# A linear-attention block and a gated mixer on one core: where two weight loads stand in the transfer queue

## The chip, the cores and the metric

The kernel runs on one core of a Trainium2 chip. It is a program for five engines that run side by side: PE (TensorE) multiplies matrices, ACT (ScalarE) evaluates functions, DVE (VectorE) works on elements, POOL (GpSimd) does small things, and SP (SyncE) issues nearly all the transfers between the chip's memory (HBM) and the core's own memory (SBUF). Engines wait for each other, and for transfers, through semaphores. The metric is the device time of one execution in microseconds, the median over the runs.

## The reference

```
h  = x + A(layernorm(x))
h2 = h + B(layernorm(h))

A:  q, k, v = x @ wqkv            # 32 heads of 16
    phi(t)  = where(t > 0, t + 1, exp(t)) + 1e-6
    kv = phi(k)^T v ;  z = sum over tokens of phi(k)      # per head
    out = (phi(q) kv / (phi(q) z + 1e-6)) @ wo

B:  z  = gelu(x @ w_in)           # w_in: 512 x 1792
    z1, z2 = the two halves of z  # 896 each
    g  = w_sp @ layernorm(z2) + b_sp     # w_sp: 2048 x 2048, mixes tokens
    out = (z1 * g) @ w_out        # w_out: 896 x 512
```

There are 2048 tokens of width 512, in bf16. The four loads that matter below are `w_in` (win, 1792 KB), `w_out` (wout, 896 KB), and the mixing weights `w_sp`, which are read transposed in 64 pieces of 128 KB.

## The kernel before

The tokens are split in 16 tiles of 128. Stage one normalises the tiles of x and transposes them: most of the transposes are transfers (`dma_t`, L673), named tx0 to tx15 after the tile. PE makes k from each pair of tiles (L756, called k4, k5 and so on), multiplies phi(k) with the normalised tile (L766) and makes q in between (L858). Stage two finishes A: it folds kv and wo in one matrix and multiplies with phi(q) (L903). Stage three normalises h, transposes it by transfers (th0 to th15, L673 again), and multiplies with win: L959 gives z2 by token tile, with its GELU on ACT (L966 or, for the tiles 0, 4, 8 and 12, L974, called g2.n), and L1013 gives z1 transposed. Stage four mixes the tokens (`mix`, L1052): for each quarter tg of the output tokens and each of 7 blocks fc of features, 16 matmuls sum over the 16 tiles of input tokens. It multiplies the result with z1 on DVE. `project` (L1072) multiplies with wout, and DVE adds h and SP stores.

The mixing weights come as transposing transfers (`load_wsp`, L1032). A piece wsp tg.st belongs to quarter tg of the output tokens and tile st of the input tokens. Quarter 0 has a semaphore for each four tiles, so that mix0.0 can go in four parts; each other quarter has one semaphore for its 16 pieces, and the first mix of that quarter waits for all of them. In `mix`, every matmul group but those of mix0.0 waits for all 16 pieces of its quarter before its first matmul. In PE's list the first such group is mix0.2.

The order of the work on each engine is not written out. `Program.schedule` is a list scheduler: it goes through the operations with an estimate of each one's duration, and on each engine takes the ready operation with the least start time plus half its `want`, a due time that comes from the table WANT (L358), one number for each operation in the order in which `build` makes them. `waits` then derives the semaphore waits. So each engine runs a fixed list in order, and an operation that waits holds up everything behind it on its engine. SP's list holds loads, transposes and stores in one queue.

In this list wout stands behind the token transpose tx8 and win behind tx15. In between and behind them stand pieces of wsp and tx12 to tx15:

```
tx8, wout, wsp0.2, tx12, tx13, tx14, tx15, win, wsp0.5, wsp0.3, wsp0.7, wsp0.4, wo, wv, ...
... th8, wsp0.14, wsp1.4, wsp0.9, wsp0.15, wsp0.10, wsp0.8, wsp1.0, wsp0.12, wsp3.10, ...
```

Of the kernel before, what the change touches and what calls it, by code (L numbers as in the profile page):

```python
# [10 lines left out]
P = 128  # L11
# [81 lines left out]
class Program:  # L93
# [306 lines left out]
def build(nc, A_x, A_wqkv, A_wo, B_w_in, B_w_sp, B_b_sp, B_w_out, out):  # L400
# [76 lines left out]
    zw = small([KD, GRAIN], BF16)  # L477
    ones = small([32], BF16)
    eps = small([4], FP32)
    mhalf = small([TPG], FP32)  # L480
    msq = small([TPG], FP32)

# [34 lines left out]
    def act_c(n, ps=True, ptr=0):  # L517
        d = (0.171 if ps else 0.2) + 0.000833 * n + 0.093 * ptr
        return d - 0.1, d + SEM
# [26 lines left out]
    for p in range(1, NP):  # L546
        load("sp", f"x{2 * p}", x[2 * p:2 * p + 2, :],
             x_dram[2 * p * P:(2 * p + 2) * P, :].rearrange("(n p) d -> p n d", p=P), 2 * P * D * 2, -28 + p)


    op("pool", pool_c(0.2), lambda e: e.memset(ident.all().ap(), 0.0), w=[ident.all()], want=-50)
# [87 lines left out]
    def T1(n):  # L639
        return 5.2 + 1.85 * n  # L640

    rs1, cT = {}, {}
    for grp in LN1:
        rs = small([len(grp)], FP32)
        nm = small([len(grp)], FP32) if any(n in ACT_NORM1 for n in grp) else None
        for n in grp:
            stats(x[n, :], Row(st_x, n), T1(n) - 4, f"st{n}")
            aggr(Row(st_x, n), 6, T1(n) - 4, f"ag{n}")
        lo, hi = grp[0], grp[-1] + 1
        for n in grp:  # L650
            if n in LATE:
                d, m = xc[n].all(), st_x[n, 6:7]
                cT[n] = Tile(XC)
                op("dve", dve_f(512), lambda e, n=n, d=d, m=m: e.tensor_scalar(d.ap(), x[n, :].ap(), m.ap(), None,
                                                                              op0=ALU.subtract),
                   r=[x[n, :], m], w=[d, cT[n]()], want=T1(n) - 3, name=f"xc{n}")
        rstd_act(st_x[lo:hi, 7], rs.all(), T1(lo) - 2.5, f"rs{lo}")
        if nm is not None:
            minus_mean(st_x[lo:hi, 6], rs.all(), nm.all(), T1(lo) - 2.5, f"nm{lo}")
        for i, n in enumerate(grp):  # L660
            rs1[n] = rs[i:i + 1]
            if n in ACT_NORM1:
                normalise_act(xn[n, :], x[n, :], nm[i:i + 1], rs[i:i + 1], T1(n) - 2, f"xn{n}")
            else:
                normalise(xn[n, :], x[n, :], st_x[n, 6:7], rs[i:i + 1], T1(n) - 2 + 4 * (n in LATE), f"xn{n}")
    load("sp", "wq", wqkv[:, 0:D], w3[:, :, 0:D], D * D * 2, 27)
    load("sp", "wv", wqkv[:, 2 * D:3 * D], w3[:, :, 2 * D:3 * D], D * D * 2, 30)
    load("sp", "wo", wo.all(), A_wo.rearrange("(c p) f -> p c f", p=P), D * D * 2, 30.1)
    load("sp", "win", win.all(), B_w_in.rearrange("(c p) f -> p c f", p=P), D * F * 2, 30.2)
    load("sp", "wout", wout.all(), B_w_out.rearrange("(c p) f -> p c f", p=P), FH * D * 2, 30.3)  # L670

    def dma_t(a, d, want, name):
        op("sp", (1.31, 2.75), lambda e: e.dma_start_transpose(d.ap(), a.ap()), r=[a], w=[d], dma=(name, False),  # L673
# [216 lines left out]
            op("dve", dve_2(1024), lambda e, r_=r_, d=d: e.tensor_tensor(d.ap(), d.ap(), r_.ap(), ALU.mult),  # L890
               r=[d, r_], w=[d], want=wd + 2, name=f"sc{gq}.{h}")

    hn_t, hn_op = {}, {}
    for p in range(NP):
        t = Tile(PS, 2)
        for ti in range(2):
# [24 lines left out]
    for grp in LN2:  # L921
# [8 lines left out]
        for i, n in enumerate(grp):  # L930
# [3 lines left out]
            else:  # L934
                hn_op[n] = normalise(t(), x[n, :], st_h[n, 6:7], rs[i:i + 1], w0 + 1 + 0.1 * i, f"hn{n}")

    def TZ(p):
        return T0 + 16 + 6 * p

    for p in range(NP):  # L940
# [11 lines left out]
        for n in (2 * p, 2 * p + 1):  # L952
            t = Tile(PS, 2)
            l = hT[:, n * P:(n + 1) * P]

            def mm(e, t=t, l=l):
                for i, (a, b) in enumerate(((FH, FH + 512), (FH + 512, F))):
                    for c in range(KD):
                        k = e.matmul(t(bank(i)).ap()[:, 0:b - a], lhsT=l.ap()[:, c, :], rhs=win[c, a:b].ap(),  # L959
                                     start=(c == 0), stop=(c == KD - 1))  # L960
                return k
            op("pe", pe_c(*([512] * 4 + [FH - 512] * 4)), mm, r=[l, win[:, FH:F]], w=[t()], want=TZ(p) + n % 2, name=f"z2.{n}",
               after=dens if n >= 2 else ())
            d = gz2[n, :]
            if n in ACT_Z:
                op("act", (act_c(FH)[0] + 0.1, act_c(FH)[1] + 0.1), lambda e, t=t, d=d, n=n: e.activation(  # L966
                    d.ap(), t(flat).ap()[:, 0:FH], ACT.Gelu_apprx_tanh, accum_out=st_z[n, 14:15].ap()), r=[t()],
                   w=[d, st_z[n, 14:15]], want=TZ(p) + 1.5, after=lnexp, name=f"g2.{n}")
                j = Tile(JK)
                op("act", (act_c(FH, ps=False)[0] + 0.1, act_c(FH, ps=False)[1] + 0.1), lambda e, d=d, n=n, j=j: e.activation(  # L970
                    j().ap(), d.ap(), ACT.Square, accum_out=st_z[n, 15:16].ap()), r=[d], w=[j(), st_z[n, 15:16]],
                   want=TZ(p) + 2, name=f"sq{n}")
            else:
                op("act", act_c(FH), lambda e, t=t, d=d: e.activation(d.ap(), t(flat).ap()[:, 0:FH], ACT.Gelu_apprx_tanh),  # L974
                   r=[t()], w=[d], want=TZ(p) + 1.5, after=lnexp, name=f"g2.{n}")
                for i, (a, b) in enumerate(((0, 512), (512, FH))):
                    s6, src = st_z[n, 6 * i:6 * i + 6], gz2[n, a:b]
                    op("dve", (0.057 + (b - a) / 985.0, 0.157 + (b - a) / 985.0 + SEM),
                       lambda e, s6=s6, src=src: e.bn_stats(s6.ap(), src.ap()), r=[src], w=[s6], want=TZ(p) + 2.5,
                       name=f"stz{n}")  # L980
                aggr(Row(st_z, n), 12, TZ(p) + 2.5, f"agz{n}")
# [43 lines left out]
    for tg in (0, 2):  # L1025
        z1_unit([(tg, KF - 1), (tg + 1, KF - 1)], z1T[KF - 1, tg * GW:(tg + 2) * GW], Z0 + 8 + tg, f"z1.{KF - 1}.{tg}")


    def load_wsp(tg, want):
        for st in range(NT):  # L1030
# [147 lines left out]
```

## Time and profile before

| | us |
|---|---|
| median of 3 runs | 242.39 |
| lowest and highest run | 242.1 and 243.06 |
| the profiled execution | 242.13 |
| its span in the trace | 240.4 |
| PE busy | 235.1 |
| DVE busy | 127.4 |
| ACT busy | 83.4 |

The span runs from the first to the last instruction of the program; what the execution took beyond it lies around the program. Busy time is the union of an engine's instructions. In a list by line, L1052 is line 1052 of the kernel; operands stand as out<-in. The timeline merges neighbouring instructions of one kind and gives their start, their length and their count; for SP, whose rows are marked SPq, the length is what the issue took, not the transfer. When a transfer is complete is given by its time from issue to landing. `wsp`, `wout`, `win`, `hT` and so on are stores in SBUF; `wqkv_wsp` holds first wqkv and wo and later the fourth quarter of the mixing weights, `k_xn_z` first k and the normalised tiles and later z2, and `xT_pq_z` first the transposed tokens and later z1.

### The profile page before, as it was taken

How to read it: one execution, taken by the hardware profiler on the slowest of the kernel's cores; microseconds unless marked ns; L12 is line 12 of the kernel's file. 1: busy time of each engine (PE TensorE's matmuls, PEld its weight loads, DVE VectorE, ACT ScalarE, POOL GpSimd, SP SyncE). 2: the span in 40 equal slices, each digit the busy share in tenths (PEclk: the TensorE clock that was granted, in tenths of full speed). 3: DMA queues.
4: the chain of work that ended last, by engine and by line, in shares of the span. 5: the costliest groups of instructions: out<-in, count | busy, mean ns of one | idle time of the engine just before them, and what ended most of it. 6: DMA issues, size and time to landing. Idle time of an engine off the chain costs nothing.

```text
span 240.4 us, 3056 instructions
## 1 busy us (share of the span) xinstructions
PE 235.1 (98%) x1177; PEld 108.6 (45%) x1199; DVE 127.4 (53%) x270; ACT 83.4 (35%) x131; POOL 14.2 (6%) x33
## 2 busy tenths in 40 slices
PE   8999999999999999999999999999999999999996
PEld 2444445444444544444444444444444444444443
DVE  5999756299999983227212333324333433332443
ACT  4898965566065799994211100000000000000000
POOL 3000000001202160213000000000000000000000
PEclk9999999999999999999999999999999999999999
DMA  6986789632632545445444544452200001000022
GB/s 195 292 206 81 206 199 313 225 102 95 173 84 56 88 100 107 91 99 100 99 97 104 83 99 108 93 107 66 87 0 0 25 22 44 0 3 0 0 87 87
DMA packets 61805, 24.18 MB, mean 101 GB/s; under 512 B 52064, under 2 KB 61152, under 8 KB 61792
## 3 DMA queue, kind: packets, MB, share of 16 engines
q1 hardware_dynamic: 61648, 23.97, 41.2%
q8 instruction: 9, 0.15, 0.3%
q10 hardware_dynamic: 144, 0.03, 0.1%
q14 instruction: 4, 0.03, 0.1%
HBM read 7.47 MB, written 2.10 MB: 40 GB/s over the span
## 4 chain that ended last, share of the span: by engine, by line
PE 94%; DVE 3%; ACT 1%; issue 1%
PE ps L1052 40%; PE ps L1072 10%; PE ps L959 10%; PE ps L1013 10%; PE ps L903 6%; PE ps L766 6%; PE ps L756 5%; PE ps L858 4%; PE ps L575 2%; DVE hT L802 1%; DVE k_xn_z L837 1%; DVE xT_pq_z L890 0%; PE ps L684 0%; DVE xT_pq_z L725 0%; PE ps L778 0%
## 5 line engine op out<-in xcount | busy, mean ns | idle before, releaser
L1052 PE MATMUL ps<-wsp,k_xn_z 128*128 128x512 bf16 x328 | 73.6, 379 | 0.4
L1058 DVE TENSOR_TENSOR e<-ps,e 128x512 bf16<-128x512 f32 x28 | 19.4, 691 | 69.2 <-PE ps L1052 69.2
L1052 PEld LDWEIGHTS ps<-wsp,k_xn_z 128*128 128x128 bf16 x336 | 32.9, 98 | 39.7
L1013 PE MATMUL ps<-hT,win 128*128 128x512 bf16 x110 | 26.0, 379 | 0.1
L959 PE MATMUL ps<-win,hT 128*128 128x384 bf16 (+1 forms) x126 | 25.3, 352 | 0.1
L1072 PE MATMUL ps<-wout,xT_pq_z 128*128 128x512 bf16 (+2 forms) x125 | 25.1, 355 | 0.1
L1052 PE MATMUL ps<-wqkv_wsp,k_xn_z 128*128 128x512 bf16 x110 | 24.2, 379 | 0.1
L1018 ACT ACTIVATE xT_pq_z<-ps 128x1024 bf16<-128x1024 f32 x14 | 14.1, 1021 | 25.5 <-PE ps L1013 25.5
L587 DVE BATCH_NORM_STATS2 small<-xh 128x6 f32<-128x512 bf16 x32 | 21.0, 679 | 3.0 <-DMA xh<-in_A_x_dram 2.9
L959 PEld LDWEIGHTS ps<-win,hT 128*128 128x128 bf16 x128 | 12.5, 98 | 12.4
L1072 PEld LDWEIGHTS ps<-wout,xT_pq_z 128*128 128x128 bf16 x126 | 11.8, 98 | 12.7
L1052 PEld LDWEIGHTS ps<-wqkv_wsp,k_xn_z 128*128 128x128 bf16 x112 | 11.0, 98 | 13.2
L1013 PEld LDWEIGHTS ps<-hT,win 128*128 128x128 bf16 x112 | 11.0, 98 | 12.6
L1076 DVE TENSOR_TENSOR e<-ps,xh 128x512 bf16<-128x512 f32 (+2 forms) x18 | 11.3, 632 | 9.7 <-PE ps L1072 9.2
L714 ACT ACTIVATE e<-ps 128x1024 bf16<-128x1024 f32 (+1 forms) x16 | 15.4, 970 | 2.0 <-PE ps L756 1.1
L766 PE MATMUL ps<-k_xn_z 128*128 128x512 bf16 x63 | 15.2, 379 | 0.2 <-issue 0.2
L858 PE MATMUL ps<-xT_pq_z,wqkv_wsp 128*128 128x512 bf16 x61 | 15.0, 379 | 0.1
L903 PE MATMUL ps<-k_xn_z,xT_pq_z 128*128 128x512 bf16 x62 | 14.0, 379 | 0.6 <-DVE k_xn_z L837 0.4
L966 ACT ACTIVATE k_xn_z<-ps 128x896 bf16<-128x896 f32 x12 | 10.9, 909 | 9.2 <-PE ps L959 9.2
L756 PE MATMUL ps<-wqkv_wsp,xT_pq_z 128*128 128x512 bf16 x55 | 13.2, 379 | 0.3 <-ACT xT_pq_z L699 0.2
L1060 DVE TENSOR_TENSOR xT_pq_z<-xT_pq_z,e 128x512 bf16<-128x512 bf16 x28 | 11.9, 425 | 2.2 <-ACT xT_pq_z L1018 1.3
L970 ACT ACTIVATE e<-k_xn_z 128x896 bf16<-128x896 bf16 x12 | 11.4, 949 | 0.3
(75 smaller groups left out, 168.6 us busy)
## 6 DMA issues: line engine op xcount, KB each, us to landing
wsp<-e SPq DMA_DIRECT2D x16, 128.0 KB
out_dram<-e SPq DMA_DIRECT2D x15, 128.0 KB, 1.7
xh<-in_A_x_dram SPq DMA_DIRECT2D x7, 256.0 KB, 3.8
win<-in_B_w_in_dram SPq DMA_DIRECT2D x1, 1792.0 KB, 7.5
wqkv_wsp<-in_A_wqkv_dram SPq DMA_DIRECT2D x3, 512.0 KB, 5.7
wout<-in_B_w_out_dram SPq DMA_DIRECT2D x1, 896.0 KB, 5.3
wsp<-in_B_w_sp_dram SPq DMA_TRANSPOSE x48, 2.7
wqkv_wsp<-in_A_wo_dram SPq DMA_DIRECT2D x1, 512.0 KB, 5.0
```

Of the source, the lines that this page charges most:

```text
L587: op("dve", (0.577, 0.69), lambda e: e.bn_stats(row[0:6].ap(), src.ap()), r=[src], w=[row[0:6]], want=want, name=name)
L714: first = op("act", act_c(n, ptr=len(pt)), lambda e: e.activation(e_(ev).ap(), src(t), ACT.Exp, scale=sc), r=[t()] + pt, w=[e_()], want=wa ...
L756: i = e.matmul(t(bank(ti)).ap(), lhsT=lhs.ap()[:, c, :], rhs=rhs.ap()[:, c, :], start=(c == 0), stop=(c == KD - 1))
L766: i = e.matmul(HT(bank(j)).ap(), lhsT=xn[n, j * P:(j + 1) * P].ap(), rhs=pk[n, :].ap(), start=(n == 0), stop=(n == NT - 1))
L858: k = e.matmul(t(bank(i)).ap(), lhsT=lhs.ap()[:, c, :], rhs=rhs.ap()[:, c, :], start=(c == 0), stop=(c == KD - 1))
L903: i = e.matmul(t(bank(ti)).ap(), lhsT=l.ap()[:, c, :], rhs=mw[c, :].ap(), start=(c == 0), stop=(c == KD - 1 and not unit))
L959: k = e.matmul(t(bank(i)).ap()[:, 0:b - a], lhsT=l.ap()[:, c, :], rhs=win[c, a:b].ap(), start=(c == 0), stop=(c == KD - 1))
L1013: k = e.matmul(t(bank(i)).ap(), lhsT=l.ap()[:, c, :], rhs=r_.ap()[:, c, :], start=(c == 0), stop=(c == KD - 1))
L1018: op("act", act_c(1024), lambda e: e.activation(d.ap(), t(None if same else flat).ap(), ACT.Gelu_apprx_tanh), r=[t()], w=[d], want=want + ...
L1052: k = e.matmul(t(bank(0)).ap(), lhsT=l.ap()[:, s - a, :], rhs=r_.ap()[:, s - a, :], start=(s == 0), stop=(s == NT - 1))
L1058: op("dve", dve_c(512), lambda e: e.tensor_tensor(gb().ap(), t(bank(0)).ap(), bsp().ap()[:, tg * GW:(tg + 1) * GW], ALU.add), r=[t(), bsp( ...
L1072: k = e.matmul(t(bank(0)).ap()[:, 0:r_.ap().shape[-1]], lhsT=l.ap()[:, fc, :], rhs=r_.ap()[:, fc, :], start=(fc == 0), stop=(fc == KF - 1))
```

## The change

Two loads get a condition beside their due time. win may be issued only when the last token tile has been normalised (xn15). wout is made at a later place in `build` and may be issued only when the GELU of token tile 8 (g2.8) is done; its number in WANT goes along unchanged. `xn_op` and `g2_op` only keep a handle on those operations.

```
-    rs1, cT = {}, {}
+    rs1, cT, xn_op = {}, {}, {}
...
-                normalise_act(xn[n, :], x[n, :], nm[i:i + 1], rs[i:i + 1], T1(n) - 2, f"xn{n}")
+                xn_op[n] = normalise_act(xn[n, :], x[n, :], nm[i:i + 1], rs[i:i + 1], T1(n) - 2, f"xn{n}")
             else:
-                normalise(xn[n, :], x[n, :], st_x[n, 6:7], rs[i:i + 1], T1(n) - 2 + 4 * (n in LATE), f"xn{n}")
+                xn_op[n] = normalise(xn[n, :], x[n, :], st_x[n, 6:7], rs[i:i + 1], T1(n) - 2 + 4 * (n in LATE), f"xn{n}")
...
-    load("sp", "win", win.all(), B_w_in.rearrange("(c p) f -> p c f", p=P), D * F * 2, 30.2)
-    load("sp", "wout", wout.all(), B_w_out.rearrange("(c p) f -> p c f", p=P), FH * D * 2, 30.3)
+    load("sp", "win", win.all(), B_w_in.rearrange("(c p) f -> p c f", p=P), D * F * 2, 30.2, after=[xn_op[NT - 1]])
...
-                op("act", act_c(FH), lambda e, t=t, d=d: e.activation(d.ap(), t(flat).ap()[:, 0:FH], ACT.Gelu_apprx_tanh),
+                g2_op[n] = op("act", act_c(FH), lambda e, t=t, d=d: e.activation(d.ap(), t(flat).ap()[:, 0:FH],
+                                                                               ACT.Gelu_apprx_tanh),
...
+    load("sp", "wout", wout.all(), B_w_out.rearrange("(c p) f -> p c f", p=P), FH * D * 2, 300.0, after=[g2_op[8]])
```

In WANT one number, 248, moves from the place of the old load to the place of the new one. SP's list becomes:

```
tx8, wsp0.2, wsp0.5, tx12, tx13, tx14, tx15, win, wsp0.3, wsp0.7, wsp0.4, wo, wv, ...
... th8, wsp0.14, wsp1.4, wsp0.9, wsp0.15, wsp0.10, wout, wsp0.8, wsp1.0, wsp0.12, wsp3.10, ...
```

More of the change, by code (lines that the diff above doesn't have):

```diff
@@ L891, in build @@
                r=[d, r_], w=[d], want=wd + 2, name=f"sc{gq}.{h}")
-    hn_t, hn_op = {}, {}
+    hn_t, hn_op, g2_op = {}, {}, {}
     for p in range(NP):
@@ L965, in build @@
             if n in ACT_Z:
-                op("act", (act_c(FH)[0] + 0.1, act_c(FH)[1] + 0.1), lambda e, t=t, d=d, n=n: e.activation(
+                g2_op[n] = op("act", (act_c(FH)[0] + 0.1, act_c(FH)[1] + 0.1), lambda e, t=t, d=d, n=n: e.activation(
                     d.ap(), t(flat).ap()[:, 0:FH], ACT.Gelu_apprx_tanh, accum_out=st_z[n, 14:15].ap()), r=[t()],
```

44 rows, old and new, of the table WANT are left out of this document.

## The prediction

> **What bounds the kernel.** I read the page's first two parts, then the chain that ended last, then SP's issue queue against PE's timeline around the two places where wout can stand.
>
> ```profile
> PE 235.1 (98%) x1177; PEld 108.6 (45%) x1199; DVE 127.4 (53%) x270; ACT 83.4 (35%) x131; POOL 14.2 (6%) x33
> PEclk9999999999999999999999999999999999999999
> PE 94%; DVE 3%; ACT 1%; issue 1%
> ```
>
> PE is busy for 235.1 of 240.4 us at the full granted clock, and it is 94% of the chain. What a moved transfer can save is therefore small, and what it can cost is the time for which PE stands still waiting for it. PE runs its list in order, so a stop in one place moves everything behind it. The profiled execution took 242.13 us, its span 240.4; the median of the runs is 242.39, so 0.26 is added to a sum on the profile.
>
> **What moves.** All of these transfers go through SP's queue. The order of work on PE, ACT, DVE and POOL is the same in both kernels; only SP's list differs. wout leaves its place behind tx8 and goes behind wsp0.10; wsp0.5 steps up from behind win to behind wsp0.2. The new condition on win (behind xn15) adds no wait: it already stands behind tx15, which waits for that operation.
>
> ```profile
> 23.84 1.27 SPq L673 DMA_TRANSPOSE xT_pq_z<-k_xn_z  x1
> 25.16 0.58 SPq L538 DMA_DIRECT2D wout<-in_B_w_out_dram  x1
> 25.78 1.24 SPq L1032 DMA_TRANSPOSE wsp<-in_B_w_sp_dram  x1
> 27.07 5.22 SPq L673 DMA_TRANSPOSE xT_pq_z<-k_xn_z  x4
> 32.33 0.58 SPq L538 DMA_DIRECT2D win<-in_B_w_in_dram  x1
> ...
> 39.73 0.58 SPq L538 DMA_DIRECT2D wqkv_wsp<-in_A_wo_dram  x1
> 40.35 0.51 SPq L538 DMA_DIRECT2D wqkv_wsp<-in_A_wqkv_dram  x1
> 44.36 16.89 SPq L884 DMA_DIRECT2D wsp<-e  x16
> 65.36 3.03 PE ps L959 x16
> win<-in_B_w_in_dram SPq DMA_DIRECT2D x1, 1792.0 KB, 7.5
> wout<-in_B_w_out_dram SPq DMA_DIRECT2D x1, 896.0 KB, 5.3
> wqkv_wsp<-in_A_wo_dram SPq DMA_DIRECT2D x1, 512.0 KB, 5.0
> wqkv_wsp<-in_A_wqkv_dram SPq DMA_DIRECT2D x1, 512.0 KB, 5.7
> ```
>
> **The early place: a gain of 0.1 us.** wout's slot of 0.62 us (25.16 to 25.78) goes and one transpose of about 1.3 us comes, so tx12 to tx15 are issued about 0.7 us later. They land no later for PE, because wout's data no longer stands ahead of them. Two answers follow, the time from issue to landing of tx12 and of tx13, the second and the third transpose behind wout (tx12 is the first of the four at 27.07, tx13 the second, at 27.07+5.22/4 = 28.4):
>
> ```profile
> DMA to landing us min/median/max: 4.4/4.4/4.4
> DMA to landing us min/median/max: 3.6/3.6/3.6
> ```
>
> ```profile
> 31.52 0.10 issue
> 31.62 1.89 PE ps L756 x8
> ...
> 34.37 0.21 PE ps L756
> ```
>
> tx12 lands at 27.07+4.4 = 31.5, and PE's k12 starts at 31.62 behind a gap of 0.10: the only gap of PE that a transfer sets here. Without wout tx12 takes about what tx8, issued at 23.84, took (first answer; the second is tx15, issued at 27.07+3*5.22/4 = 31.0):
>
> ```profile
> DMA to landing us min/median/max: 2.5/2.5/2.5
> DMA to landing us min/median/max: 2.9/2.9/2.9
> ```
>
> So it lands at 27.07+0.7+2.5 = 30.3, and the 0.10 goes. tx15, last of the four, lands at 31.0+0.7+2.9 = 34.6 at the latest; its matmuls are the second four of the eight whose chain begins at 34.37, so they start at 34.37+4*0.216 = 35.2 (1.89 us for eight is 0.216 each and the last one's drain). That cover is about 0.6 us. Bounds of the early place: -0.1 and, if this cover fails, +0.3. I take -0.1. win is issued 0.7 us later, at 33.0; it took 7.5 us and is first read at 65.36. wo and wv follow one transpose fewer, so no later than now. At 44.36 SP waits for ACT (its last issue ended at 40.86), so from there on its queue stands as before: 3.5 us hide the shift.
>
> **The late place: PE waits.** From 102.43 SP issues the mixing weights with no pause, and the issue interval is the transposes' pace.
>
> ```profile
> 102.43 10.78 SPq L1032 DMA_TRANSPOSE wsp<-in_B_w_sp_dram  x8
> ...
> 107.94 0.92 ACT L974 ACTIVATE k_xn_z<-ps 128x896 bf16<-128x896 f32 x1
> 115.31 3.62 PE L1052 MATMUL ps<-wsp,k_xn_z 128*128 128x512 bf16 x16
> ```
>
> The eight are wsp0.14, 1.4, 0.9, 0.15, 0.10, 0.8, 1.0, 0.12. wout comes in ahead of wsp0.8, so at 108.9. Its new condition, the GELU of token tile 8 on ACT, ends at 107.94+0.92 = 108.86; SP reaches wout when its transpose ends, at about 108.9, so the wait costs nothing, but only just: whatever makes that GELU later holds all the transposes behind it.
>
> PE's mix0.2 (the 16 matmuls at 115.31) is the first that needs the third and fourth quarters of wsp0, so wsp0.8 and wsp0.12. Those are the first and the third transpose behind wout. Here are the rows of wsp0.8 and wsp0.12 as they are now:
>
> ```profile
> L1032 SPq DMA_TRANSPOSE wsp<-in_B_w_sp_dram x1: 1647/1647/1647, 108.9 to 108.9; - x1
> DMA to landing us min/median/max: 2.9/2.9/2.9
> ...
> L1032 SPq DMA_TRANSPOSE wsp<-in_B_w_sp_dram x1: 1267/1267/1267, 111.9 to 111.9; - x1
> DMA to landing us min/median/max: 2.7/2.7/2.7
> ```
>
> wsp0.12 lands at 111.9+2.7 = 114.6, 0.7 us before PE wants it. wout's issue alone takes 0.62 of that. Its 896 KB take the rest and more, and nothing behind mix0.2 in PE's list can go ahead of it.
>
> The price comes from wout itself at its old place. Its third follower, tx13, was issued at 28.4 and landed 3.6 later, at 32.0: 6.8 us after wout's issue. From 108.95 this gives 115.75. From a landing to the first matmul takes 0.15 us (tx12 at 27.07+4.4 = 31.47, k12 at 31.62), so mix0.2 starts at 115.9 and not at 115.31: **+0.59**. That is one bound. The other counts from the landing ahead of wout. tx8 landed at 23.84+2.5 = 26.3, tx13 5.7 us behind it. wsp0.10, ahead of the new place, lands late:
>
> ```profile
> L1032 SPq DMA_TRANSPOSE wsp<-in_B_w_sp_dram x1: 1267/1267/1267, 107.6 to 107.6; - x1
> DMA to landing us min/median/max: 3.3/3.3/3.3
> ```
>
> It lands at 110.9, so wsp0.12 at 116.6 and mix0.2 at 116.75: **+1.4**. Between the two I choose by wsp0.8's row: its issue took 1647 ns where its neighbours take 1267, so at exactly this place SP's queue is held for 0.38 us, and wout will meet that hold. That makes 0.59+0.38 = **+0.97**.
>
> [...]
>
> **Behind that.** Everything else moves by about 0.6 us or by PE's own stop, and is covered:
>
> ```profile
> 136.03 29.52 PE L1052 MATMUL ps<-wsp,k_xn_z 128*128 128x512 bf16 x133
> 171.42 13.98 PE L1052 MATMUL ps<-wsp,k_xn_z 128*128 128x512 bf16 x62
> L1032 SPq DMA_TRANSPOSE wsp<-in_B_w_sp_dram x1: 1261/1261/1261, 135.1 to 135.1; - x1
> 162.84 2.56 SPq L1032 DMA_TRANSPOSE wqkv_wsp<-in_B_w_sp_dram  x2
> 167.81 70.97 SPq L1079 DMA_DIRECT2D out_dram<-e  x17
> ```
>
> wsp1's last transpose is issued at 135.1 and takes some 2.7 to land, as wsp0.12 does (137.8); PE needs it after 24 of the 133 matmuls, at 136.03+24*0.216 = 141.2. Cover: 3.4 us. wsp2 is all issued before 162.84, and PE reads it from 171.42. The first store is issued at 167.81, behind DVE, when SP has been free since 165.4. wout itself is read from 165 on and lands near 115.
>
> **Sum.** 242.13 - 0.10 + 0.97 = 243.0 on the profile, and 243.3 on the median. That is +0.36%, inside the 0.5% (1.21 us) that a measurement of this kernel can tell from no change.
>
> **Rivals.** *PE does not wait.* [...] Chance 0.16.
>
> *A longer stop, slower than the bound.* Just before wout's new place a block of program code is fetched on the same DMA engines:
>
> ```profile
> q8 instruction: 1, 0.02, 6.0%
> L1032 SPq DMA_TRANSPOSE wsp<-in_B_w_sp_dram x1: 1263/1263/1263, 106.3 to 106.3; - x1
> DMA to landing us min/median/max: 4.2/4.2/4.2
> ```
>
> The first row is of the window 108 to 109, the others are wsp0.15, in flight then: 4.2 us against the 2.7 of a transpose next to nothing, so 1.5 lost. If the fetch falls on wout or its followers instead of ahead of them, the stop grows to 0.97+1.5 = 2.5 and the time to 244.5, on the median 244.8. It decides when the fetch comes after wout's issue at 108.95; now it comes in the us before. Against it: PE's program and its pace up to there are the same. Chance 0.22, in which I also put a wait on the late GELU.
>
> *Faster.* The early stage had 0.62 us of issue and 896 KB of traffic less. But PE has only 5.3 us of gaps in all, and one of 0.10 ends with a transfer; a gain over 1.21 us has no place to come from. Best case 242.0. Chance 0.04.
>
> **Chances and range.** The forecast (a stop between 0.5 and 1.6 us, on the median 242.8 to 243.9) has 0.58; of that I put 0.17 above the bound of +1.21 and 0.41 within it. Faster 0.04; same 0.41+0.16 = 0.57; slower 0.17+0.22 = 0.39. The range runs from the no-wait case with the spread of the runs, 242.2, to the long stop, 244.7.
>
> **What would show it.** In the changed kernel's profile: SP issues wout near 108.9 and wsp0.8 about 0.6 later; wout lands near 114.5; wsp0.12 near 116; PE's timeline shows, between the 16 matmuls of L1013 and the 16 of the mixing line, an idle stretch of about 1 us, the largest after PE's start; the chain names a transfer or "issue" there, or DVE no longer alone beside PE. Before 108 PE's starts lie about 0.1 us earlier, the gap at 31.52 gone; behind mix0.2 all lies later by one constant. The prediction is wrong if that stretch is missing or above 1.6 us, if SP stands before wout waiting for ACT, or if PE waits at mix1.6 too.

## The result, and the profile after

| | before | after |
|---|---|---|
| median of 8 runs each, us | 242.6 | 243.82 |
| lowest and highest run, us | 241.78 and 243.25 | 243.27 and 245.09 |
| span of the profiled execution, us | 240.4 | 241.5 |

The ratio of after to before is 1.0065, with a 95% interval of 1.0044 to 1.0087: slower by some 1.6 us (1.1 to 2.1); the medians differ by 1.22. That lies about at the 0.5% (1.21 us) which the prediction took as its bound, with the interval reaching to both sides of it, and at the upper end of its likeliest case (242.8 to 243.9).

PE decides again. Here are its busy time, its clock, the shares of the chain that ended last, and the costliest group, from the page of the changed kernel, and behind them the same group before. A group's row ends with its busy time in us and the mean of one in ns, and then the idle time before it with what ended it.

```profile
PE 236.4 (98%) x1199; PEld 108.5 (45%) x1199; DVE 127.5 (53%) x270; ACT 83.4 (35%) x131; POOL 14.2 (6%) x33
PEclk9999999999999999999999999999999999999999
PE 67%; DVE 18%; SPq 10%; DMA 2%; ACT 1%; issue 1%; POOL 1%
L1056 PE MATMUL ps<-wsp,k_xn_z 128*128 128x512 bf16 x336 | 74.2, 379 | 1.3 <-DMA wsp<-in_B_w_sp_dram 1.3
```

```profile
L1052 PE MATMUL ps<-wsp,k_xn_z 128*128 128x512 bf16 x328 | 73.6, 379 | 0.4
```

Before, the mixing group showed 0.4 us of idle time and no transfer as its cause. Now it is 1.3 us, all of it ended by the landing of a piece of wsp, and the chain that ended last runs through SP and a transfer and no longer nearly all through PE. (The trace before has 1177 matmuls beside 1199 weight loads, that of the changed kernel 1199 of each, so some matmul records are missing from the trace before.)

The place in PE's timeline of the changed kernel, and then SP's queue in front of it with the GELU of tile 8 on ACT:

```profile
111.51 3.62 PE L1016 MATMUL ps<-hT,win 128*128 128x512 bf16 x16
116.43 3.61 PE L1056 MATMUL ps<-wsp,k_xn_z 128*128 128x512 bf16 x16 [1.31 <-DMA wsp<-in_B_w_sp_dram]
```

```profile
103.24 6.19 SPq L1036 DMA_TRANSPOSE wsp<-in_B_w_sp_dram  x4
109.48 0.58 SPq L539 DMA_DIRECT2D wout<-in_B_w_out_dram  x1
110.11 3.84 SPq L1036 DMA_TRANSPOSE wsp<-in_B_w_sp_dram  x3
107.59 0.92 ACT L976 ACTIVATE k_xn_z<-ps 128x896 bf16<-128x896 f32 x1
```

Queued, mix0.2 would have started 16 matmuls of 0.216 us behind 111.51, at 114.96. It started at 116.43, so the stop moved everything by 1.47 us. The row says 1.31 because it counts from the end of the last matmul before, 111.51+3.62 = 115.13, and in a queue the next one starts 0.16 us ahead of that end. In what follows "idle" is the row's number; the loss is 0.16 more.

wsp0.12 is the transpose that ended it; here are its rows, asked for alone, and its place in the chain that ended last:

```profile
L1036 SPq DMA_TRANSPOSE wsp<-in_B_w_sp_dram x1: 1262/1262/1262, 112.7 to 112.7; - x1
  PE ps L1056: 1.3, 1
DMA to landing us min/median/max: 3.7/3.7/3.7
```

```profile
112.69 3.65 DMA wsp<-in_B_w_sp_dram
116.34 0.09 issue
```

It landed at 116.34, 6.9 us behind wout's issue, where the prediction had 6.8. And at the early place the gap in front of k12 is gone. In the chain of the changed kernel there, k12 (the eight matmuls at 31.43) follows the four ahead of it with no gap:

```profile
30.56 0.86 PE ps L767 x4
31.43 1.73 PE ps L757 x8
33.15 0.86 PE ps L767 x4
34.02 1.73 PE ps L757 x8
```

### The profile page after: what moved, and what is told of

It reads as the page before. It is cut to its first block, busy times and chain, and to the rows that moved or that the text cites. A ratio compares the mean times of both kernels' runs of the same rounds, so it can differ in the third digit from the quotient of the medians.

```text
span 241.5 us, 3078 instructions
## 1 busy us (share of the span) xinstructions
PE 236.4 (98%) x1199; PEld 108.5 (45%) x1199; DVE 127.5 (53%) x270; ACT 83.4 (35%) x131; POOL 14.2 (6%) x33
## 4 chain that ended last, share of the span: by engine, by line
PE 67%; DVE 18%; SPq 10%; DMA 2%; ACT 1%; issue 1%; POOL 1%
PE ps L1056 39%; PE ps L1076 10%; SPq L1036 7%; PE ps L767 6%; PE ps L757 5%; DVE small L589 5%; PE ps L859 4%; DVE xh L917 3%; SPq L674 3%; DVE hn L616 2%; DVE xT_pq_z L891 2%; DMA wsp<-in_B_w_sp_dram 2%; PE ps L1016 1%; DVE xT_pq_z L726 1%; DVE small L593 1%
## 5 line engine op out<-in xcount | busy, mean ns | idle before, releaser
L961 PE MATMUL ps<-win,hT 128*128 128x512 bf16 (+1 forms) x128 | 25.4, 352 | 0.0
L904 PE MATMUL ps<-k_xn_z,xT_pq_z 128*128 128x512 bf16 x64 | 14.5, 379 | 0.4 <-DVE k_xn_z L838 0.4
```

Source lines behind the costliest of these rows:

```text
L904: i = e.matmul(t(bank(ti)).ap(), lhsT=l.ap()[:, c, :], rhs=mw[c, :].ap(), start=(c == 0), stop=(c == KD - 1 and not unit))
```

## The experiments

Theory A is that of the prediction: wout's bytes stand ahead of wsp0.8 and wsp0.12 in the queue, this alone stops PE at mix0.2, and the early place gives back a little. Its rivals: B, what counts is that SP is held there (by the condition on wout, or beside a fetch of program code) and not the bytes; C, a part of the loss lies elsewhere.

Most kernels below move wout in SP's finished list and leave the lists of the other engines as they are:

```
+def place(g, name, before, free=True):
+    sp = g.order["sp"]
+    o = next(o for o in sp if o.name == name)
+    sp.remove(o)
+    if free:
+        o.deps = {}
+    sp.insert(next(i for i, q in enumerate(sp) if q.name == before), o)
+    for i, q in enumerate(sp):
+        q.pos = i
...
     g.schedule()
+    place(g, "wout", "wsp3.10")
     fillers(g)
```

Ratios are to the kernel before on the same chip, with 95% intervals. Where a row counts fewer than the 16 matmuls of mix0.2, the stretch of the timeline that was asked for ends there; its start is not touched by that.

**wout behind wsp0.12.** The edit is the one above.

> Only wout's place in SP's list differs from the changed kernel: behind wsp0.12 instead of ahead of wsp0.8, without its condition. Theory A (wout's data stands ahead of wsp0.8 and wsp0.12 in the transfer queue, and this alone stops PE at mix0.2; the early place gives a gain): the stop of 1.47 us at mix0.2 goes and the early gain of about 0.35 stays, so a span of 240.0 to 240.1 against 240.4 before, a time 0.3 us below before. Theory C (part of the loss lies elsewhere behind mix0.2, from the transposes being late): a span above 240.4. wsp1's last piece should land near 138.4 with no stop at mix1.6 under A.

Measured: 242.02 against 242.18 us, ratio 0.9995 (0.9973 to 1.0017), span 240.2. PE's timeline:

```profile
111.64 3.62 PE L1016 MATMUL ps<-hT,win 128*128 128x512 bf16 x16
115.10 3.19 PE L1056 MATMUL ps<-wsp,k_xn_z 128*128 128x512 bf16 x14
```

The stop is gone, and with it the whole loss. So the loss came from the order of these few transfers, and C has nothing to explain. The pieces of the later quarters are as late as in the changed kernel (the first, wsp3.10, is issued at 113.99 in both), and no one waits for them.

**wout where SP stands idle.** `place(g, "wout", "th12")`.

> wout goes where SP stands idle, behind th0 and ahead of th12, without its condition. Theory A: no stop at mix0.2, early gain kept, span 240.0 to 240.1. Rival: wout, though SP is idle there, delays th12 to th15 and so z2.12 on PE; then a gap of PE near 80 us and a span of 240.4 or more.

Measured: 242.45 against 242.18 us, ratio 1.0003 (0.998 to 1.0027). No stop at mix0.2: the sixteen matmuls ahead of it start at 112.59, and it at 116.04, 3.45 behind them. The span of this profile is 241.1 all the same, and its cause stands ahead of wout, which is issued at 70.5:

```profile
57.79 3.62 PE L904 MATMUL ps<-k_xn_z,xT_pq_z 128*128 128x512 bf16 x16
62.46 3.63 PE L904 MATMUL ps<-k_xn_z,xT_pq_z 128*128 128x512 bf16 x16 [1.05 <-DVE xT_pq_z L891]
```

PE waited for DVE where A's output is made (L904), a stop of which the other profiles show nothing or, once, 0.9. So one span can be 1 us off for reasons that have nothing to do with where wout stands. From here on a stop is read at its own place, and the verdict on the time comes from the runs.

**mix0.2 in four parts.** It waits for the third and fourth quarters only in front of the matmuls that read them.

```
-        parts = [(0, NT)] if (tg, fc) != (0, 0) else [(i, i + 4) for i in range(0, NT, 4)]
+        parts = [(0, NT)] if (tg, fc) not in ((0, 0), (0, 2)) else [(i, i + 4) for i in range(0, NT, 4)]
...
```

> The changed kernel with mix0.2 cut in four groups of four matmuls, as mix0.0 is, so that only the third and the fourth group wait for the quarters of wsp0 that come behind wout; four matmuls of z1 go in between. Theory A: wsp0.8 lands at 115.3 and wsp0.12 at 116.3 while PE reaches these groups at about 117.5 and 118.4, so the stop goes: span 240.0 to 240.1. Theory C: the loss is not only this wait, and a span above 240.4 remains.

Measured: 242.2 against 242.18 us, ratio 1.0001 (0.9977 to 1.0025). wout stays at the changed kernel's place, the transposes behind it land as late after their issue as there (5.2, 4.4 and 3.7 us), and no stop is left:

```profile
117.14 1.03 PE L1056 MATMUL ps<-wsp,k_xn_z 128*128 128x512 bf16 x4
118.00 1.03 PE L1016 MATMUL ps<-hT,win 128*128 128x512 bf16 x4
118.86 3.40 PE L1056 MATMUL ps<-wsp,k_xn_z 128*128 128x512 bf16 x14
```

This shows the other half of the mechanism: the late pieces cost time only because mix0.2 asks for all sixteen before its first matmul. (The scheduler also put four matmuls of z1 behind the first part, at 118.00; they are 0.86 us of the cover.) The span of this profile, 242.2, is again off for a reason of its own, in the first 11 us; it is told at the end.

**The late place alone.** wout is loaded twice, where the kernel before loads it (`twice` puts a copy of the load there) and where the changed kernel does, and wsp0.5 goes back.

```
+    place(g, "wsp0.5", "wsp0.3")
+    twice(g, "wsp0.2")
```

> The late place alone: wout is loaded where the kernel before loads it, wsp0.5 is back at its old place too, and wout is loaded a second time at the changed kernel's place. Theory A: the early gain is gone and the stop stays: span 240.4+1.47 = 241.9, time 1.5 us above before. If the early gain is nothing but scatter between two profiles: span 241.5 as the changed kernel.

Measured: 243.39 against 242.18 us, ratio 1.0042 (1.0016 to 1.0069), span 241.2. Slower, by the late place alone. The stop is smaller than expected, 0.76 us idle, and the early gap is back:

```profile
30.43 1.03 PE L767 MATMUL ps<-k_xn_z 128*128 128x512 bf16 x4
31.53 1.89 PE L757 MATMUL ps<-wqkv_wsp,xT_pq_z 128*128 128x512 bf16 x8
116.15 3.18 PE L1056 MATMUL ps<-wsp,k_xn_z 128*128 128x512 bf16 x14 [0.76 <-DMA wsp<-in_B_w_sp_dram]
```

From 30.43 to 31.53 is 1.10 us for four matmuls that take 0.86 when queued: 0.24 lost to the wait for tx12. Before it was 0.26 (30.50 to 31.62); with wout gone from there it is 0. So the early gain is real, some 0.25 us, but none of the kernels that have it without the stop came out measurably faster than before.

**Fewer bytes.** Three of wout's seven chunks stay at the late place; four go ahead of th12.

```
-    load("sp", "wout", wout.all(), ...
+    w_o = B_w_out.rearrange("(c p) f -> p c f", p=P)
+    load("sp", "wout", wout[0:3, :], w_o[:, 0:3, :], 3 * P * D * 2, 300.0, after=[g2_op[8]])
+    load("sp", "wout2", wout[3:KF, :], w_o[:, 3:KF, :], 4 * P * D * 2, 300.0, after=[g2_op[8]])
...
+    place(g, "wout", "wsp0.8")
+    place(g, "wout2", "th12")
```

> Only three of wout's seven chunks (384 of 896 KB) stand at the changed kernel's place; the other four go into SP's idle stretch ahead of th12. Theory A (bytes ahead in the queue set the stop): 512 KB less at the 385 GB/s that wout's stream shows is 1.36 us less, then the issue of wsp0.12 is the later bound (112.7+2.7 = 115.4), so the stop falls from 1.47 to 0.4 or 0.5, span about 240.5. Theory B (what stops PE is that SP is held at that place, by the condition and by the fetch of program code, not the bytes): the stop stays near 1.4, span 241.4.

Measured: 242.15 against 242.45 us, ratio 0.9982 (0.9955 to 1.0009). (The span of this profile is 241.0; a wait of 0.83 us for a token transpose at 12.98, far ahead of both of wout's places, lifts it.)

```profile
112.23 3.62 PE L1016 MATMUL ps<-hT,win 128*128 128x512 bf16 x16
115.93 2.32 PE L1058 MATMUL ps<-wsp,k_xn_z 128*128 128x512 bf16 x10
109.08 1.53 SPq L539 DMA_DIRECT2D wout<-in_B_w_out_dram  x1
```

112.23+3.45 = 115.68, so the loss is 0.25 us. SP is held here as well, for about 1 us on wout's issue (1.53 us, where that of all seven chunks takes 0.58), and yet the stop nearly goes: the bytes decide it, and B falls in its strong form. What is left is the hold. wsp0.12, asked for alone, is issued at 113.2 and lands 2.7 us later, as in the kernel before:

```profile
DMA to landing us min/median/max: 2.7/2.7/2.7
```

**More bytes.** Behind wout another 768 KB are copied into the store of the normalised h, which no one reads any more at that time.

```
+    load("sp", "spare", hn_v.all(), B_w_out.rearrange("(c p) f -> p c f", p=P)[:, 0:6, :], 6 * P * D * 2, 300.0,
+         after=[o for o in g.ops if o.name in [f"th{n}" for n in range(NT)]])
...
+    place(g, "wout", "wsp0.8")
+    place(g, "spare", "wsp0.8", False)
```

> Behind wout, at the same place, 768 KB more are copied into a store that nothing reads any more. Theory A: at 385 GB/s 2.0 us more, so a stop of about 3.5 us and a span of 243.5. Theory B: one or two more issue slots, 0.6 to 0.9 us, span 242.1 to 242.4.

Measured: 247.27 against 242.45 us in four runs, ratio 1.0202 (1.0158 to 1.0245). The timeline, and PE's busy time and granted clock in three stretches (columns: PE, PEld, DVE, ACT, POOL busy with the count of instructions, clock, share of the DMA engines, GB/s):

```profile
119.02 5.01 PE L1059 MATMUL ps<-wsp,k_xn_z 128*128 128x512 bf16 x16 [3.05 <-DMA wsp<-in_B_w_sp_dram]
```

```profile
118.50:121.50 3.00, 2.48 (x6) 0.90 (x7) 0.00 (x0) 0.00 (x0) 0.00 (x0) 0.50 0.49 107
121.50:122.00 0.50, 0.50 (x3) 0.23 (x2) 0.00 (x0) 0.00 (x0) 0.00 (x0) 0.62 0.97 222
122.00:126.00 4.00, 4.00 (x20) 1.79 (x19) 1.11 (x2) 1.02 (x1) 0.00 (x0) 1.00 0.44 100
```

The stop is 3.05 us idle, a loss of 3.2 where 3.5 was expected. But the time rose by 4.9. One more piece is in the same row: half a us before the stop ends the clock falls to 0.50, it is full again from about 121.9, and the sixteen matmuls take 5.01 instead of 3.61: 1.4 us more. What is left of the 4.9, 0.3 us, is less than single profiles differ by (this one has the wait of 0.9 us for DVE that was mentioned above).

**Further ahead.** `place(g, "wout", "wsp0.14")`, eight transposes ahead of mix0.2's last one.

> wout goes five transposes earlier, right behind th8, without its condition. Theory A: the copy's data still stands ahead of the same transposes, but each of the five in between takes SP about 1.3 us to issue and the queue only about 0.55 us to move, so the queue has recovered when wsp0.8 comes; what stays is wout's issue of 0.62 us, and wsp0.12 lands near 114.9: a stop of 0 to 0.3 us, span 240.1 to 240.4. If a copy delays all transposes behind it by its own length for good: the stop stays at 1.5, span 241.5.

Measured: 242.81 against 242.45 us, ratio 1.0011 (0.998 to 1.0041). No stop:

```profile
112.25 3.62 PE L1016 MATMUL ps<-hT,win 128*128 128x512 bf16 x16
115.70 2.54 PE L1056 MATMUL ps<-wsp,k_xn_z 128*128 128x512 bf16 x11
```

The queue catches up: SP issues a transpose each 1.3 us, and behind wout they land 0.5 to 0.6 us apart (115.3, 115.8 and 116.3 in the changed kernel). Here the first behind wout lands 5.1 us after its issue and wsp0.12, the eighth, 2.7 after its own, as before the change. Issued at 112.9, it lands at 115.6, so that about 0.1 us is to spare.

**Without the condition.** `place(g, "wout", "wsp0.8")`, which keeps the place and drops the wait for the GELU of tile 8.

> The changed kernel with the condition on wout (GELU of tile 8) taken away, its place in SP's list kept. Theory A: SP reaches wout only when the issue of wsp0.10 ends (109.4), after that GELU, so nothing changes: span 241.4 to 241.6. Theory B: wout is issued earlier, by up to 0.5 us, and the stop shrinks by as much.

Measured: 243.68 against 242.45 us, ratio 1.0055 (1.0033 to 1.0077): as the changed kernel. The condition costs nothing; in the changed kernel that GELU ended at 107.59+0.92 = 108.5, and SP came to wout at 109.48. But the stop is 1.79 us idle here, and SP's queue shows why:

```profile
116.92 2.32 PE L1056 MATMUL ps<-wsp,k_xn_z 128*128 128x512 bf16 x10 [1.79 <-DMA wsp<-in_B_w_sp_dram]
103.49 6.31 SPq L1036 DMA_TRANSPOSE wsp<-in_B_w_sp_dram  x4
109.84 0.58 SPq L539 DMA_DIRECT2D wout<-in_B_w_out_dram  x1
```

Four transposes take 5.17 us to issue elsewhere; ahead of wout they took 6.31 here and 6.19 in the changed kernel. In the changed kernel SP is held inside the issue of wsp0.10, which took 2.28 us where 1.26 is usual, so for 1.0 us; here the four are 1.1 longer. In the changed kernel a packet of 0.02 MB moves meanwhile in the queue that the trace names `q8 instruction`, at 107.9; it is read here, as in the prediction, as a fetch of program code. Its row in the window 107.5 to 108.5:

```profile
q8 instruction: 1, 0.02, 7.1%
```

In the kernel with the late place alone the four took 5.17, the hold fell on wout's own issue (0.82 us for 0.58), and the stop was 0.76. So two pictures seemed possible for one order. The last four runs look at that and at the places around.

**The changed kernel again, twice.** No edit.

> The changed kernel once more, to see how its stop scatters. In three profiles with wout at this place the hold of SP by the fetch of program code fell on the issue of wsp0.10 (stops of 1.3 and 1.8 us) or on wout's own (0.8). Expected: one of these two pictures again, SP's long issue (over 2 us) at wsp0.10 with a stop of 1.2 to 1.9, or a normal one with a stop of 0.6 to 1.0. A stop outside both would say that something else decides it.

> As the run before it: the changed kernel, either a long issue of wsp0.10 and a stop of 1.2 to 1.9 us, or a normal one and a stop of 0.6 to 1.0.

Measured: 242.55 and 243.21 us, a single run each, beside 242.1 of the kernel before. The first:

```profile
103.14 5.17 SPq L1036 DMA_TRANSPOSE wsp<-in_B_w_sp_dram  x4
108.37 0.91 SPq L539 DMA_DIRECT2D wout<-in_B_w_out_dram  x1
115.73 2.53 PE L1056 MATMUL ps<-wsp,k_xn_z 128*128 128x512 bf16 x11 [0.77 <-issue]
```

The second:

```profile
103.27 6.11 SPq L1036 DMA_TRANSPOSE wsp<-in_B_w_sp_dram  x4
109.43 0.58 SPq L539 DMA_DIRECT2D wout<-in_B_w_out_dram  x1
116.39 1.89 PE L1056 MATMUL ps<-wsp,k_xn_z 128*128 128x512 bf16 x8 [1.23 <-DMA wsp<-in_B_w_sp_dram]
```

Both pictures, from one program. The size of the stop goes with the issue on which the hold falls: 0.8 us idle where it is wout's own, 1.2 to 1.8 where it is that of wsp0.10 before it. The fetch itself is no later in one than in the other: it begins 0.6 to 0.7 us into the issue of wsp0.10 in both (between 107.6 and 107.7, and between 107.8 and 107.9), and why the hold falls on one issue or on the next is open. This is what is left of B. It may be a part of the spread of the runs; that was not tried.

**Two transposes earlier, one later.** `place(g, "wout", "wsp0.15")` and `place(g, "wout", "wsp1.0")`.

> wout two transposes earlier than in the changed kernel, ahead of wsp0.15, without its condition; wsp0.12 is then the fifth transpose behind it. Theory A with recovery: wout issued near 105.9, landed 111.3 to 112.8 depending on the fetch of program code that falls into its stream, wsp0.12 at 115.3 to 115.5 by its own issue, so a stop at mix0.2 of 0.3 to 0.5 us, between the 0 with eight transposes in between and the 0.8 to 1.8 with three. If the stop depends only on wout being ahead at all: 0.8 to 1.8.

> wout one transpose later than in the changed kernel, behind wsp0.8, without its condition; only wsp1.0 and wsp0.12 follow it before mix0.2. Theory A: wsp0.8 lands on its own near 112, wout is issued near 110.4 and wsp0.12, the second behind it, lands about 6.3 us later at 116.7: a stop of 1.3 to 2.0 us, not less than in the changed kernel. If the stop grew with the number of needed pieces behind wout (two there, one here): about half of it, 0.4 to 0.9.

Measured, a single run each: 242.54 and 244.95 us beside 242.1. Five transposes behind wout:

```profile
115.73 2.53 PE L1056 MATMUL ps<-wsp,k_xn_z 128*128 128x512 bf16 x11 [0.44 <-issue]
```

Two transposes behind wout:

```profile
118.16 2.10 PE L1056 MATMUL ps<-wsp,k_xn_z 128*128 128x512 bf16 x9 [2.19 <-issue]
```

With eight, five, three and two transposes from wout to wsp0.12 the idle time is 0, 0.44, 0.76 to 1.79, and 2.19, and with wout behind it 0 again. It does not halve when only one of the two needed quarters stands behind wout; it grows. There is less time to catch up (wsp0.12 lands 4.3 us after its issue there, and 3.7 or 3.8 with three in between), and the hold comes on top. (The 2.19 is above what was expected by 0.2: SP's hold fell ahead of wout there too, with 2.43 us for the issue of wsp0.8. With five in between wsp0.12 still lands 3.8 after its issue, but there the fetch falls among the five, at 111.0, so this run says little of how fast the queue catches up.)

No version beats the kernel before by more than its interval. The nearest, with fewer bytes at the late place, is at 0.9982 (0.9955 to 1.0009).

## Why the prediction was right or wrong

**The bound, and what moves.** Right. PE's list is the same, its clock is full, and the loss is one stop in it. In the changed kernel's profile all of PE from mix0.2 on is 1.12 us later (115.31 to 116.43), as its span is.

**The early place.** Right in kind, too small: the term of -0.10 measured -0.26. The step took the gap of the chain, 0.10, for what PE lost there. From the start of the four matmuls ahead (30.50) to k12 (31.62) it was 1.12 us where 0.86 is the queue's pace. The gap as shown counts from the end of the last matmul and so leaves out the same 0.16 us as at the stop.

**The condition on wout costs nothing.** Right, shown by the run without it.

**The late place.** Right in mechanism and place. The price by wout's own old record held well: the third transpose behind it landed 6.8 us after its issue at the old place and 6.9 at the new one. What was mis-sized is the hold of SP. The prediction took 0.38 us from the row of wsp0.8; in the three profiles of the changed kernel it is 0.33 us where it fell on wout's issue, and 1.0 and 0.9 where it fell on that of wsp0.10 before it. So the stop is not one number: 0.97 us were forecast, and the loss was 1.47, 0.93 and 1.39 (the idle time and 0.16). The forecast fits the one profile whose hold had the assumed size; the other two lie at the upper bound of 1.4.

**Behind it.** Right: PE has no wait behind mix0.2 in any profile of the changed kernel.

**The sum.** 243.3 was forecast and 243.82 measured; the range held it. The point value of the ratio passed the bound of 0.5%, for which the text had given 0.39 and not the most. In the terms of the first profile the sum should read -0.26 and +1.47, not -0.10 and +0.97: +1.2. The two errors have opposite signs, so the sum is off by less than the stop is. The +1.2 is what the medians differ by (1.22) and lies within the interval of 1.1 to 2.1 from the ratio; whether the executions that were not profiled had longer stops can't be told from these runs. (The range ends at 244.7, a little below the 244.8 that the text gives for its own long stop.)

**The rivals.** That PE would not wait fell: the copy took as long as at its old place, 5.4 us from issue to landing where it had been 5.3. No run with all of wout at this place and mix0.2 in one part shows the start without a wait from which the range begins, at 242.2; in the three profiles of the changed kernel PE stood idle at mix0.2 for 1.31, 0.77 and 1.23 us. The longer stop by a fetch of program code fell in its size (2.5 us, 244.8), and its condition, a fetch behind wout's issue, was not met in the three profiles of the changed kernel: the fetch begins 0.7 to 1.6 us ahead of it (at 107.9 in the first, with wout's issue at 109.48). It did not fall in its kind: in each of the three a fetch falls in the issue of wsp0.10, which is the held one or the one ahead of it.

## What to carry to other kernels

In this in-order transfer queue the place of a load that no one needs for another 50 us was not free: count how many issues lie from such a load to the first transfer that someone waits for, and how much each of them lets the queue catch up. Here eight transposes repaid a copy of 896 KB, with about 0.1 us to spare, and three did not (0.76 to 1.79 us idle). With the place unchanged, cutting the consumer's wait in parts, so that each part asks only for what it reads, removed the stop as well.

## What the runs showed of the hardware that was not expected

A stop of PE cost more than its length here: in the run with more bytes 3.2 us, and 1.4 more in the sixteen matmuls behind it. In that run, with a rest of 3.05 us, the granted clock was 0.97 in 118.0 to 118.5, 0.50 for the 3 us behind that, and 0.62 in the half us from 121.5: half speed for about 3.4 us. The same was seen in the first microseconds of the run with mix0.2 in four parts, after a rest of only 1.13 us; here are PE's timeline and the clock by stretch of that run:

```profile
6.70 0.40 PE L685 MATMUL ps<-small,hn 128*128 128x128 bf16 x4 [1.13 <-DVE hn L656]
7.32 3.50 PE L746 MATMUL ps<-wqkv_wsp,hn 128*128 128x512 bf16 x8 [0.22 <-DMA wqkv_wsp<-in_A_wqkv_dram]
```

```profile
7.00:7.50 0.50, 0.28 (x3) 0.13 (x2) 0.50 (x3) 0.37 (x1) 0.00 (x0) 0.92 1.03 358
7.50:10.50 3.00, 3.00 (x8) 1.06 (x7) 2.35 (x9) 1.79 (x5) 0.00 (x0) 0.50 1.27 298
10.50:11.00 0.50, 0.50 (x6) 0.39 (x5) 0.50 (x2) 0.00 (x0) 0.00 (x0) 0.67 1.06 237
```

Eight matmuls took 3.50 us, where the same eight took 1.94 in the kernel before. That is most of why this profile's span is 242.2 and its execution took 243.96, where the median of these runs is 242.2. By these stretches the slow time is about 3.4 us in both. Rests of 1.2 to 2.2 us at mix0.2 set off nothing: the mean clock is 1.0 in two profiles of the changed kernel (idle for 1.31 and 1.23 us), of the run without the condition (1.79) and of that with two transposes behind wout (2.19). What decides is open.

The fetch of program code, as the queue `q8 instruction` is read here, is the other surprise: nine packets with 0.15 MB in all in the span, before and after the change. Around the one near mix0.2 (at 108.6 before, at 107.9 in the changed kernel) the transpose that is in flight lands 1.5 us late in both (4.2 us for wsp0.15, where 2.7 is usual), and an issue of SP beside it takes longer: by 0.38 us before (wsp0.8, 1647 ns where its neighbours take 1267) and by 1.0 in the changed kernel (wsp0.10, 2282 ns where 1262 is usual). In the other runs with wout near that place the hold lies between 0.2 us (the late place alone) and 1.2 (two transposes behind wout). That this packet and a late issue stand together is seen in the profiles before and after; that the one causes the other was not tried.
